# A new opening for a fused layer norm, long convolution and feed-forward kernel: first tile and first weights loaded first, roots on GpSimd, constant matmuls in early waits

## The chip, the cores and the metric

The kernel runs on one core of a Trainium2 chip. A core has five engines with queues of their own, each of which works strictly in the order in which instructions were put there: TensorE (PE: matmuls, with PEld for the loading of their weights), VectorE (DVE), ScalarE (ACT), GpSimd (POOL) and SyncE (SP, which here only issues DMAs). Engines wait for one another by semaphores. The metric is the device time of one execution in microseconds (us), the median of several.

## The reference

With S = 2048 rows, D = 1024 columns and F = 3584 hidden columns:

```python
x = A_q                                  # 2048 x 1024
xn = (x - mean(x)) / sqrt(var(x) + 1e-5) # per row
# branch A, per column of D
k_shift = causal_conv(k, shift_k)        # 4 taps
kv = k_shift * v
y = causal_conv(kv, ssm_k) + kv * ssm_D  # 2048 taps, by FFT in the reference
# branch B
h = silu(xn @ w1)                        # 2048 x 3584
return x + xn * y + h @ w2
```

All inputs and the output are float32.

## The kernel before, in words

Both products of branch B run on TensorE in float16, each operand split into a high and a low half, with three matmuls for each pair of blocks (high x high, high x low, low x high; `steps`, L959, and `steps2`, L1091). A split (`split`, L365) is two operations: ACT writes the high half (scaled, `a_act`, L350), and DVE subtracts it from the source and writes the low half (`v_stt`, L346). The first product uses Strassen-like sums of row and column quarters: an operand is either a plain quarter (A11, A12, A21, A22) or a sum of quarters (S1 to S4 for rows, T1 to T4 for weights). The convolution of branch A is done by Fourier matrices on TensorE, with the transforms in between on DVE, after the opening that concerns us here.

The rows come in 16 tiles of 128 rows. Tiles 0 to 3 are A11 and A12, tiles 4 to 7 are A21 and A22. A tile passes these steps:

- `load_row` (L503) loads it, the first two tiles in two pieces of 256 KB each.
- `ln_rows` (L512) takes statistics on DVE (two `bn_stats`, one `bn_aggr` per tile), the root of the variance on ACT (`AF.Sqrt`, L537), a chain of five small DVE operations that makes one refined reciprocal root (L530 to L534), and the norm itself, one DVE operation of 128x1024 per tile (L543). Statistics are taken for groups of 2, 2, 4 and 8 tiles before the group's root.
- `transposes` (L549) turns it on TensorE, four blocks of 128x128 into a PSUM tile of the ring `ft` (three tiles), and `first_rows`, `keep`, `lower_sums` and `upper_sums` split and add what came out, on ACT and DVE.

The weights w1 come in pairs of 256 hidden columns. `load_pair` (L711) loads one, `scales_w1` (L733) takes its sum of squares on ACT (`AF.Square` with an accumulator, into `junk`), adds the partitions by a matmul with ones (`total`, L444, PSUM tile `nm`), and makes powers of two from the sum as scales: for the first two pairs in a chain of six DVE operations (`norm`, L457, with `then`, L749), for the later ones with ACT adding up the columns, two DVE operations, and two small ACT operations for the scales (`norm_act`, L479). `factors_w1` (L781) splits the scaled weights into the places `wo`.

`feed_forward` (L1050) orders the matmuls. It begins with `plain_unit` (L970) for pair 0 with the upper rows, in two groups of two tiles (256 columns of the moving operand); then pair 1 with the upper rows, then pairs 0 and 1 with the lower rows, which need tiles 4 to 7 complete; then the units of sums. A SiLU on ACT takes each result out of PSUM. The SiLU and the root belong to different activation tables, and a change of table is an instruction of its own on ACT (`ACT_TABLE_LOAD`).

Nothing of this order is written out by hand. Each activity is a generator that yields operations (`Op`) with an engine, an estimated duration and a margin. `Order.run` (L165) keeps an estimated clock per engine and always emits the operation with the earliest estimated start, less a bias of its stream. The engines then run that order as emitted. A few matmuls with zeros (`op.fill`) are put into estimated TensorE gaps after 45 us of the estimate. The opening is set by `begin` (L1797): row tiles 0 and 1, weight pair 0, row tiles 2 and 3, pair 1, row tiles 4 to 7. `warm_up` (L1823) yields 26 matmuls of constants in float32, two records each in the profile, with an estimate of 0.44 us each, and holds a tile of the ring `ft` until they are emitted.

Of the kernel before, what the change touches and what calls it, by code (L numbers as in the profile page):

```python
# [11 lines left out]
F32 = mybir.dt.float32  # L12
# [8 lines left out]
P = 128  # L21
# [84 lines left out]
class Order:  # L106


# [56 lines left out]
    def run(self):  # L165
        while self.streams:
# [125 lines left out]
def h3_ffn_kernel(ctx, tc, x, kp, vs, fs, shift, dskip, w1, w2, cfwd, cinv, out):  # L292
# [151 lines left out]
    def total(ring, ss, n, margin):  # L444
# [7 lines left out]
        def mm():  # L452
            nc.tensor.matmul(pt[:, 0:n], onesb, high, start=True, stop=True)
        yield T(mm, pt[:, 0:n], [ss], 0.12, m=margin)
# [24 lines left out]
    def norm_act(ring, ss, ns, then, flags, margin=1.5):  # L479

        cols = len(ns)
        pt, tok, e, etok = yield from total(ring, ss, sum(ns), margin)
# [3 lines left out]
        tok.set()  # L486
        power, inverse = e[:, 0:cols], e[:, 2:2 + cols]

        def chain():
            nc.vector.tensor_scalar(power.bitcast(I32), power.bitcast(I32), 24, 23,  # L490
                                    op0=ALU.logical_shift_right, op1=ALU.logical_shift_left)
            nc.vector.reciprocal(inverse, power)
        yield V(chain, e, [power], us=0.33)
# [18 lines left out]
    def ln_rows():  # L512
        for t0, n, bias in ((0, 2, 0.26), (2, 2, 0.17), (4, 4, 0.15), (8, 8, 0.03)):
            yield bias
            q = slice(t0, t0 + n)
            mv = lnp.tile([P, 2, 8], F32, name="mv", bufs=2)
            m = mv[:, :, 0:n]
# [10 lines left out]
            def chain(m=m, q=q):  # L528
                v = stat[:, q, 1]
                nc.vector.reciprocal(m[:, 0, :], m[:, 0, :])  # L530
# [3 lines left out]
                nc.vector.tensor_mul(rstd[:, q], m[:, 0, :], m[:, 1, :])  # L534
# [4 lines left out]
            p.writes += [m[:, 0, :], m[:, 1, :]] + ([nmr] if n == 8 else [])  # L539
            yield p  # L540
            for t in order_in:
                xt = xts[t][0]
                yield V(lambda: nc.vector.tensor_scalar(xt, xt, stat[:, t, 0:1], rstd[:, t:t + 1], op0=SUB, op1=MUL),  # L543
# [189 lines left out]
    def scales_w1():  # L733
        for n, (_, i) in enumerate(pairs):
# [14 lines left out]
            def then(e, i=i):  # L749
                sc = wsc[:, i]  # L750
                nc.vector.tensor_scalar(sc[:, 3:5], powers[:, 3:5], e, None, op0=MUL)
                nc.vector.reciprocal(e, e)
                nc.vector.tensor_scalar(sc[:, 0:3], powers[:, 0:3], e, None, op0=MUL)

# [215 lines left out]
    def plain_unit(i, b, xf, ready, m=1, free=False):  # L970
# [921 lines left out]
```

## Time and profile before

| | |
|---|---|
| median of 3 runs | 1251.88 us (1251.4 to 1251.94) |
| profiled execution | 1250.78 us, span 1249.0 us |
| TensorE busy | 1227.0 us, 98% of the span |
| DVE busy | 1127.2 us, 90% |
| ACT busy | 749.5 us, 60% |
| GpSimd busy | 132.9 us, 11% |
| mean granted TensorE clock | 0.997 |

The span runs from the first to the last instruction of the profiled execution. A row of the profile in order of time reads: start, duration, engine, line of the kernel, operation, written tile <- read tiles, their shapes, how often in a row, and in brackets how long the engine had been idle before and who released it. A line is often that of a helper: L355 is every ACT operation, L347 every combined DVE operation, so the names of tiles tell more (`xt` row tiles, `x` places of the transposed rows and of the first weight pairs, `wo` split weights, `ff` results in PSUM, `mv` and `rstd` the root, `pow` and `wsc` the scales of w1, `junk` the squares).

### The profile page before, as it was taken

What the parts mean: (1) busy time and instruction counts of PE and PEld (TensorE: products, weight loads), DVE (VectorE), ACT (ScalarE), POOL (GpSimd) and SP (SyncE); (2) the same over time, 40 slices, a digit from 0 to 9 for tenths busy, and PEclk for the clock granted to TensorE, in tenths of its full rate; (3) what the DMA queues carried; (4) which work ended last, traced back from release to release, by engine and by line L of the source; (5) the groups of instructions that cost most, each with busy time, mean ns of one, the idle gap of its engine ahead of it and who ended that gap; (6) DMA issues with size and microseconds to landing.
All of it is one profiled execution on the core that took longest, in us unless ns stands there. A gap on an engine that the chain in (4) does not pass through costs nothing.

```text
span 1249.0 us, 17052 instructions
## 1 busy us (share of the span) xinstructions
PE 1227.0 (98%) x6017; PEld 591.7 (47%) x6017; DVE 1127.2 (90%) x1390; ACT 749.5 (60%) x1309; POOL 132.9 (11%) x141
## 2 busy tenths in 40 slices
PE   7899999999999999999999999999999999999998
PEld 6444544444444454445444544544454454445444
DVE  7999997889799979999899799889979979998992
ACT  6868897878767786757762632563273264526231
POOL 0000000000000030001110300310030030113114
PEclk8999999999999999999999999999999999999999
DMA  9358999889999898978998897689586587978766
GB/s 336 94 176 289 314 309 309 276 277 349 321 332 299 263 260 272 258 239 230 345 329 213 178 266 176 149 245 276 127 199 184 131 169 245 250 157 143 161 144 93
DMA packets 254293, 292.93 MB, mean 235 GB/s; under 512 B 48768, under 2 KB 167808, under 8 KB 252032
## 3 DMA queue, kind: packets, MB, share of 16 engines
q1 hardware_dynamic: 227472, 266.93, 67.4%
q0 software_dynamic: 26736, 24.92, 14.9%
q8 instruction: 47, 0.77, 0.2%
q14 instruction: 38, 0.31, 0.1%
HBM read 193.22 MB, written 98.57 MB: 234 GB/s over the span
## 4 chain that ended last, share of the span: by engine, by line
PE 69%; DVE 20%; issue 4%; DMA 4%; ACT 2%; POOL 0%; SPq 0%; DVEq 0%; POOLq 0%; ACTq 0%
PE ff L1096 10%; PE ff L1098 10%; PE ff L1097 10%; PE ff L966 10%; PE ff L964 10%; PE ff L965 10%; DVE spec L344 7%; DVE tmp L344 3%; DVE x L347 2%; PE ps L1563 2%; PE ps L1565 2%; PE ps L1564 2%; DVE spec L347 1%; DVE ht L347 1%; DMA out<-yt 1%
## 5 line engine op out<-in xcount | busy, mean ns | idle before, releaser
L1096 PE MATMUL ff<-x,wo 128*128 128x512 f16 x868 | 328.1, 378 | 1.0 <-DVE hf L347 0.6
L1098 PE MATMUL ff<-x,wo 128*128 128x512 f16 x868 | 328.1, 378 | 0.0
L1097 PE MATMUL ff<-x,wo 128*128 128x512 f16 x868 | 328.1, 378 | 0.0
L965 PE MATMUL ff<-x,wo 128*128 128x512 f16 (+1 forms) x808 | 303.9, 376 | 2.7 <-DVE x L347 2.7
L964 PE MATMUL ff<-x,wo 128*128 128x512 f16 (+1 forms) x808 | 303.9, 376 | 2.2 <-ACT wo L355 1.5
L966 PE MATMUL ff<-x,wo 128*128 128x512 f16 (+1 forms) x808 | 303.8, 376 | 1.7 <-DVE wo L347 0.9
L344 DVE TENSOR_TENSOR spec<-spec 128x1024 f32<-128x1024 f32 (+2 forms) x272 | 263.2, 1000 | 2.3
L1098 PEld LDWEIGHTS <-wo 128*128 128x128 f16 x868 | 84.9, 98 | 101.5
L1096 PEld LDWEIGHTS <-wo 128*128 128x128 f16 x868 | 84.9, 98 | 100.7
L1097 PEld LDWEIGHTS <-wo 128*128 128x128 f16 x868 | 84.9, 98 | 100.7 <-issue 1.4
L966 PEld LDWEIGHTS <-wo 128*128 128x128 f16 x808 | 79.4, 98 | 98.3 <-issue 3.3
L964 PEld LDWEIGHTS <-wo 128*128 128x128 f16 x808 | 79.4, 98 | 90.7 <-ACT wo L355 1.7
L965 PEld LDWEIGHTS <-wo 128*128 128x128 f16 x808 | 79.4, 98 | 88.5 <-issue 1.1
L341 POOL DMA_DIRECT2D out<-hf x59 | 52.2, 885 | 449.4 <-ACT hf L355 363.4
L355 ACT ACTIVATE hf<-ff,invc 128x512 f32<-128x512 f32 x60 | 40.9, 682 | 97.8 <-PE ff L1098 68.5
L341 POOL DMA_DIRECT2D out<-yt x56 | 63.1, 1327 | 333.1 <-DVE yt L347 189.6
L344 DVE TENSOR_TENSOR tmp<-spec 128x2048 f32<-128x2048 f32 (+1 forms) x48 | 92.6, 1934 | 0.9
L347 DVE SCALAR_TENSOR_TENSOR ht<-hf,wsc,ht 128x1024 f16<-128x1024 f32 (+1 forms) x56 | 67.3, 1204 | 12.5 <-ACT ht L355 12.4
L355 ACT ACTIVATE spec<-spec 128x1024 bf16<-128x1024 f32 x32 | 33.8, 1055 | 70.7 <-DVE spec L344 70.6
L347 DVE SCALAR_TENSOR_TENSOR wo<-raw,wsc,wo 128x512 f16<-128x512 f32 (+1 forms) x56 | 56.6, 1014 | 11.3 <-ACT wo L355 10.9
L355 ACT ACTIVATE spec<-ps 128x512 f32<-128x512 f32 x96 | 55.3, 590 | 16.6 <-PE ps L1565 14.9
L355 ACT ACTIVATE ht<-hf,wsc 128x1024 f16<-128x1024 f32 (+1 forms) x56 | 60.7, 1085 | 4.4 <-DVE hf L344 3.0
(173 smaller groups left out, 1753.6 us busy)
## 6 DMA issues: line engine op xcount, KB each, us to landing
wo<-hs SPq DMA_DIRECT2D x160, 256.0 KB, 3.7
hs<-ht SPq DMA_DIRECT2D x80, 256.0 KB, 4.6
wraw<-in_w SPq DMA_DIRECT2D x31, 512.0 KB, 5.3
out<-hf POOLq DMA_DIRECT2D x59, 256.0 KB, 4.3
raw<-in_w SPq DMA_DIRECT2D x28, 512.0 KB, 6.0
kin<-in_kp SPq DMA_DIRECT2D x16, 704.0 KB, 5.6
kf<-in_fs SPq DMA_DIRECT2D x8, 1024.0 KB, 5.3
hsfS<-ht SPq DMA_DIRECT2D x32, 256.0 KB, 4.5
```

Source lines behind the costliest of these rows:

```text
L341: return Op("POOL", 1.1, 4.8, lambda: nc.gpsimd.dma_start(o, i, accum_op=ADD), [i], [o], m, n)
L344: return V(lambda: nc.vector.tensor_tensor(o, a, b, op=op), o, [a, b], **k)
L347: return V(lambda: nc.vector.scalar_tensor_tensor(o, a, s, b, op0=op0, op1=op1), o, [a, b] + ([] if isinstance(s, float) else [s]), **k)
L355: nc.scalar.activation(o, i, func, scale=scale, **kw)
L964: nc.tensor.matmul(o, w[:, 0, k], xf[:, :, k, 0], start=first and k == 0, stop=False, **kw)
L965: nc.tensor.matmul(o, w[:, 0, k], xf[:, :, k, 1], start=False, stop=False, **kw)
L966: nc.tensor.matmul(o, w[:, 1, k], xf[:, :, k, 0], start=False, stop=last and k == KH - 1, **kw)
L1096: nc.tensor.matmul(o, hx[:, n, 0, :], wc[:, n, 0, q], start=first and n == 0, stop=False, **kw)
L1097: nc.tensor.matmul(o, hx[:, n, 0, :], wc[:, n, 1, q], start=False, stop=False, **kw)
L1098: nc.tensor.matmul(o, hx[:, n, 1, :], wc[:, n, 0, q], start=False, stop=last and n == 3, **kw)
L1563: nc.tensor.matmul(o, cf[:, 0], hi[i], start=i == 0, stop=False, **kw)
L1564: nc.tensor.matmul(o, cf[:, 0], lo[i], start=False, stop=False, **kw)
```

## The change

- **Loads.** `begin` loads row tile 0, then weight pair 0, then row tiles 1, 2 and 3. The rest is as before.
- **Row norms.** The groups are now 1, 1, 2, 4 and 8 tiles. The root and the five DVE operations are replaced by two GpSimd operations: add 1e-5, then raise to the power -0.5. For the groups of 2 and 4 two more GpSimd operations make -mean x rstd, and the tiles 3, 5 and 7 are normed by one ACT operation (`Identity` with scale and bias) in place of the DVE one.
- **Table.** No root is left on ACT, and the first activation loads the table of the SiLU.
- **Scales of w1.** Pairs 0 to 3 take `norm_act` with `joined`: TensorE also adds up the columns (a first matmul with 1e-32, then one for each column), so that neither DVE nor ACT has to, and the two DVE operations read PSUM directly. The margin of that matmul in the estimate goes from 1.5 to 0.5. Pairs 0 and 1 leave the DVE chain of six and get their scales from two ACT operations.
- **First unit.** `plain_unit` for pair 0 with the upper rows runs in groups of 1, 1 and 2 tiles (128, 128 and 256 columns) in place of 2 and 2.
- **Warm-up.** Its tile comes from the ring `ff`. The estimate for one warm-up matmul is 0.3 us. After the 26, every estimated gap of TensorE is filled with bfloat16 matmuls of constants of 512 columns (`order.spare`), until the first product has been emitted (`flag["first"]`).

```diff
@@ class Order, run
-            if op.fill is not None and t > 45.0:
+            if self.spare is not None and op.eng == "PE":
+                for _ in range(int((t - self.free["PE"] - 0.1) / 0.22)):
+                    self.spare()
+            elif op.fill is not None and t > 45.0:
@@ constants
+    tinyb = cst.tile([P, 1], BF16, name="tinyb")
+    nc.vector.memset(tinyb, 1e-32)
-    eps = cst.tile([P, 1], F32, name="eps")
-    nc.vector.memset(eps, 1e-5)
+    half = cst.tile([P, 1], F32, name="half")
+    nc.vector.memset(half, -0.5)
@@ def total(ring, ss, n, margin, joined=False):
         def mm():
-            nc.tensor.matmul(pt[:, 0:n], onesb, high, start=True, stop=True)
-        yield T(mm, pt[:, 0:n], [ss], 0.12, m=margin)
+            if joined:
+                nc.tensor.matmul(pt[:, 0:1], onesb, tinyb, start=True, stop=False)
+                for q in range(n):
+                    nc.tensor.matmul(pt[:, 0:1], onesb, high[:, q:q + 1], start=False, stop=q == n - 1)
+            else:
+                nc.tensor.matmul(pt[:, 0:n], onesb, high, start=True, stop=True)
+        yield T(mm, pt[:, 0:n], [ss], 0.12 + 0.04 * n * joined, m=margin)
@@ def norm_act(ring, ss, ns, then, flags, margin=1.5, joined=False):
-        for c, m in enumerate(ns):
+        for c, m in enumerate(() if joined else ns):
             o = pt[:, sum(ns[:c]):sum(ns[:c]) + m]
             yield a_act(o, o, AF.Copy, bias=1e-30, total=e[:, c:c + 1])
+        sums = pt[:, 0:cols] if joined else power
         def chain():
-            nc.vector.tensor_scalar(power.bitcast(I32), power.bitcast(I32), 24, 23,
+            nc.vector.tensor_scalar(power.bitcast(I32), sums.bitcast(I32), 24, 23,
                                     op0=ALU.logical_shift_right, op1=ALU.logical_shift_left)
             nc.vector.reciprocal(inverse, power)
@@ def ln_rows():
-        for t0, n, bias in ((0, 2, 0.26), (2, 2, 0.17), (4, 4, 0.15), (8, 8, 0.03)):
+        for t0, n, bias in ((0, 1, 0.26), (1, 1, 0.26), (2, 2, 0.17), (4, 4, 0.15), (8, 8, 0.03)):
             def chain(m=m, q=q):
-                v = stat[:, q, 1]
-                nc.vector.reciprocal(m[:, 0, :], m[:, 0, :])
-                nc.vector.tensor_mul(m[:, 1, :], m[:, 0, :], m[:, 0, :])
-                nc.vector.scalar_tensor_tensor(m[:, 1, :], v, 1e-5, m[:, 1, :], op0=ADD, op1=MUL)
-                nc.vector.tensor_scalar(m[:, 1, :], m[:, 1, :], -0.5, 1.5, op0=MUL, op1=ADD)
-                nc.vector.tensor_mul(rstd[:, q], m[:, 0, :], m[:, 1, :])
-                if n == 8:
-                    nc.vector.scalar_tensor_tensor(nmr, stat[:, :, 0], -1.0, rstd, op0=MUL, op1=MUL)
-            yield a_act(m[:, 0, :], stat[:, q, 1], AF.Sqrt, bias=eps)
-            p = V(chain, rstd[:, q], [stat[:, q, :], m[:, 0, :]], us=0.8)
+                nc.gpsimd.tensor_scalar(m, stat[:, q, 1], 1e-5, None, op0=ADD)
+                nc.gpsimd.tensor_tensor(rstd[:, q], m, power, op=ALU.pow)
+                if n in (2, 4):
+                    nc.gpsimd.tensor_scalar(m, stat[:, q, 0], -1.0, None, op0=MUL)
+                    nc.gpsimd.tensor_tensor(nmr[:, q], m, rstd[:, q], op=MUL)
+            power = half.to_broadcast([P, n])
+            p = V(chain, rstd[:, q], [stat[:, q, :]], us=1.2)
+            p.eng = "POOL"
+            if n in (2, 4):
+                p.busy += 0.5
             yield p
+            if n == 8:
+                yield V(lambda: nc.vector.scalar_tensor_tensor(nmr, stat[:, :, 0], -1.0, rstd, op0=MUL, op1=MUL),
+                        nmr, [stat, rstd])
             for t in order_in:
                 xt = xts[t][0]
+                if t in (3, 5, 7):
+                    yield a_act(xt, xt, AF.Identity, rstd[:, t:t + 1], nmr[:, t:t + 1])
+                    flag["xn", t].set()
+                    continue
@@ def scales_w1():
-            if n < 2:
-                yield from norm(ctxs["nm"], ss[:, 0:m], (m,), then, ([wsc[:, i]], [flag["scaled", n], tok]))
-            else:
-                yield from norm_act(ctxs["nm"], ss[:, 0:m], (m,), scales, [flag["scaled", n], tok])
+            early = n < 4
+            yield from norm_act(ctxs["nm"], ss[:, 0:m], (m,), scales, [flag["scaled", n], tok],
+                                0.5 if early else 1.5, early)
@@ def feed_forward():
-        yield from plain_unit(0, 0, first, (r, r), 2)
+        yield from plain_unit(0, 0, first, (r, r), (1, 2, 4))
@@ def begin():
-        for t in (0, 1):
-            yield from load_row(t)
+        yield from load_row(0)
         yield from load_pair(0)
-        for t in (2, 3):
+        for t in (1, 2, 3):
             yield from load_row(t)
@@ def warm_up():
-        pt, tok = ft.tile([P, KH, P])
+        pt, tok = ff.tile([P, 4, P])
         for _ in range(26):
-            yield T(lambda: nc.tensor.matmul(pt[:, 0, :], ones, ones, start=True, stop=True), pt[:, 0, :], [], 0.44)
+            yield T(lambda: nc.tensor.matmul(pt[:, 0, :], ones, ones, start=True, stop=True), pt[:, 0, :], [], 0.3)
+        def constants():
+            nc.tensor.matmul(pt.rearrange("p a b -> p (a b)"), onesb, oneb.to_broadcast([P, W]), start=True, stop=True)
+        order.spare = constants
+        yield flag["first"]
+        order.spare = None
         tok.set()
@@ start
-    nc.scalar.activation(warm, ones[:, 0:1], AF.Sqrt)
+    nc.scalar.activation(warm, ones[:, 0:1], AF.Silu)
+    order.table = AF.Silu
```

More of the change, by code (lines that the diff above doesn't have):

```diff
@@ L106 @@
 class Order:
+    spare = None
     def __init__(self):
@@ L477, in norm, with norm_act @@
             t.set()
-    def norm_act(ring, ss, ns, then, flags, margin=1.5):
+    def norm_act(ring, ss, ns, then, flags, margin=1.5, joined=False):
         cols = len(ns)
-        pt, tok, e, etok = yield from total(ring, ss, sum(ns), margin)
-        for c, m in enumerate(ns):
+        pt, tok, e, etok = yield from total(ring, ss, sum(ns), margin, joined)
+        for c, m in enumerate(() if joined else ns):
             o = pt[:, sum(ns[:c]):sum(ns[:c]) + m]
             yield a_act(o, o, AF.Copy, bias=1e-30, total=e[:, c:c + 1])
-        tok.set()
+        if not joined:
+            tok.set()
         power, inverse = e[:, 0:cols], e[:, 2:2 + cols]
+        sums = pt[:, 0:cols] if joined else power
         def chain():
-            nc.vector.tensor_scalar(power.bitcast(I32), power.bitcast(I32), 24, 23,
+            nc.vector.tensor_scalar(power.bitcast(I32), sums.bitcast(I32), 24, 23,
                                     op0=ALU.logical_shift_right, op1=ALU.logical_shift_left)
             nc.vector.reciprocal(inverse, power)
-        yield V(chain, e, [power], us=0.33)
+        yield V(chain, e, [sums], us=0.33)
+        if joined:
+            tok.set()
         yield from then(power, inverse)
@@ L968, in steps, with plain_unit @@
                     skip_group_check=more)
-    def plain_unit(i, b, xf, ready, m=1, free=False):
+    def plain_unit(i, b, xf, ready, ends=(4,), free=False):
         ph = []
@@ L975, in plain_unit @@
             ph.append(ff.tile([P, 4, P]))
-        for n, j in [(n, j) for n in range(m) for j in range(2)]:
-            q = slice(n * 4 // m, (n + 1) * 4 // m)
+        for q, j in [(slice(([0] + list(ends))[n], e), j) for n, e in enumerate(ends) for j in range(2)]:
+            last = q.stop == 4
             for a in range(2):
-                for r in ready[a][n * len(ready[a]) // m:(n + 1) * len(ready[a]) // m]:
+                for r in ready[a] if len(ends) == 1 else ready[a][q]:
                     yield r
@@ L983, in plain_unit @@
                 yield from steps(ph[j][0][:, q, :], w, xf[a][:, q], a == 0, a == 1)
-                if free and n == m - 1:
+                if free and last:
                     tok.set()
-            if n == m - 1:
+                flag["first"].set()
+            if last:
                 if j == 0:
```

14 lines of the change are left out of this document (5 added, 9 removed).

## The prediction

> **What bounds the kernel now.** I read the page's shares first, then the busy time by stretches of the span, then the order of time in the first 54 us, then the groups of ScalarE (ACT) there.
>
> ```profile
> PE 1227.0 (98%) x6017; PEld 591.7 (47%) x6017; DVE 1127.2 (90%) x1390; ACT 749.5 (60%) x1309; POOL 132.9 (11%) x141
> ```
>
> Busy time of each engine in five stretches that I cut at the places the argument needs (columns: stretch, its length, then PE, PEld, DVE, ACT, POOL busy with instructions, granted clock, DMA share, GB/s), and two finer ones:
>
> ```profile
> 0.00:13.10 13.10, 9.49 (x65) 9.16 (x65) 7.39 (x26) 6.00 (x14) 0.69 (x6) 1.00 0.84 290
> 13.10:53.90 40.80, 31.80 (x206) 21.26 (x207) 37.41 (x81) 34.71 (x65) 0.00 (x0) 0.92 0.66 230
> 53.90:550.00 496.10, 495.78 (x2367) 231.76 (x2367) 451.11 (x580) 381.21 (x636) 11.46 (x11) 1.00 0.88 281
> 550.00:1200.00 650.00, 646.19 (x3143) 306.54 (x3142) 604.46 (x675) 314.98 (x576) 103.44 (x107) 1.00 0.80 208
> 1200.00:1249.00 49.00, 43.69 (x239) 23.00 (x236) 26.85 (x33) 12.57 (x20) 17.32 (x18) 0.99 0.67 108
> 15.00:20.00 5.00, 2.73 (x13) 1.64 (x14) 4.51 (x9) 4.42 (x10) 0.00 (x0) 0.54 1.03 419
> 20.00:25.00 5.00, 5.00 (x38) 4.20 (x37) 4.51 (x14) 2.17 (x5) 0.00 (x0) 0.78 1.02 406
> ```
>
> From 53.9 to 1200 us TensorE idles 0.32 + 3.81 = 4.1 us in 1146. So the end is, to a first reading, the moment at which TensorE starts to run without gaps, plus a fixed amount of matmul work. The opening is different: to 53.9 us TensorE idles 3.6 + 9.0 us, 8 us of the rest are warm-up matmuls, and around 15 to 22 us its clock is granted at half. What it waits for is ACT and VectorE (DVE):
>
> ```profile
> 1.07 7.99 PE L1827 MATMUL ft<-one 128*128 128x128 f32 x52 [1.07 <-DVE one L395]
> 10.90 1.50 PE L562 MATMUL ft<-ident,xt 128*128 128x128 f32 x12 [1.84 <-issue]
> 12.24 0.17 PE L453 MATMUL nm<-ss,oneb 128*128 128x4 bf16 x1
> 16.36 0.40 PE L964 MATMUL ff<-x,wo 128*128 128x256 f16 x1 [1.48 <-ACT wo L355]
> 20.84 0.42 PE L965 MATMUL ff<-x,wo 128*128 128x256 f16 x1
> 21.06 0.42 PE L966 MATMUL ff<-x,wo 128*128 128x256 f16 x1
> 22.60 0.27 PE L966 MATMUL ff<-x,wo 128*128 128x256 f16 x1
> 22.71 0.27 PE L964 MATMUL ff<-x,wo 128*128 128x256 f16 x1
> 53.99 0.38 PE L965 MATMUL ff<-x,wo 128*128 128x512 f16 x1 [0.67 <-DVE x L347]
> ```
>
> The last row is the start of the gapless part: the first product with the lower rows (tiles 4 to 7), held up by their last split on DVE. The first useful matmul is at 16.36. In the stretch 13.1 to 53.9 DVE is busy 37.4 of 40.8 us and ACT 34.7, so both queues are nearly full, and ACT's 6.1 us of idle time are these two groups' (columns: instructions, busy, mean | idle before, releaser):
>
> ```profile
> L355 ACT ACTIVATE x<-ft 128x512 f16<-128x512 f32 x14 | 8.2, 601 | 4.2 <-PE nm L453 2.8 <-DVE s L344 1.3
> L355 ACT ACTIVATE xt<-ft 128x512 f32<-128x512 f32 x8 | 4.7, 602 | 1.8 <-DVE x L347 1.8
> L355 ACT ACT_TABLE_LOAD x3 | 3.8, 1283 | 0.1
> L355 ACT ACTIVATE junk<-x 128x1024 bf16<-128x1024 f32 x2 | 2.1, 1050 | 0.0
> L355 ACT ACTIVATE ht<-hf,wsc 128x1024 f16<-128x1024 f32 x1 | 1.2, 1151 | 0.0
> L355 ACT ACTIVATE mv<-stat,eps 128x2 f32<-128x2 f32 (+1 forms) x2 | 0.6, 290 | 0.0
> ```
>
> **The change, part by part.** I price it at one place: how much earlier the 53.99 row comes.
>
> *Loads.* Each queue entry stays; only SP's order changes. Row tile 1 (two 256 KB pieces) moves behind the four pieces of the w1 pair, and everything after these keeps its place.
>
> ```profile
> 3.48 0.69 DVE L524 BATCH_NORM_STATS2 st<-xt 128x6 f32<-128x512 f32 x1 [2.38 <-DMA xt<-in_x]
> 6.29 1.40 DVE L524 BATCH_NORM_STATS2 st<-xt 128x6 f32<-128x512 f32 x2 [0.99 <-DMA xt<-in_x]
> 8.05 0.63 ACT L355 ACTIVATE junk<-x 128x512 bf16<-128x512 f32 x1 [5.81 <-DMA x<-in_w]
> 9.79 0.16 DVE L534 TENSOR_TENSOR rstd<-mv 128x2 f32<-128x2 f32 x1
> 10.90 0.19 ACT L355 ACTIVATION_READ_ACCUMULATOR junk<-x 128x1 f32 x1
> ```
>
> The third piece now lands at 6.29, the fifth at 8.05. So w1 is there from about 6.3 on, and four squares of 0.8 us (0.63 + 0.19) end near 9.7 where they ended at 11.1. Tile 1 lands two to three us later and is normed about a microsecond later than now, tile 0 three earlier.
>
> *First matmul.* Tile 0 is normed by about 7.1, but the 26 warm-ups still hold TensorE until 9.06. The plan believes 0.3 us each, so 7.8 in all, and puts some constant matmuls of 0.22 us before the first product (no row shows how many; I take ten, from a planned gap of some 2 us). Transposes of tile 0 (8 of 0.125 us, from the row of twelve) then end near 10.6, the sum (five small matmuls for the one at 12.24) near 11.0, its two DVE operations near 11.4, two scales on ACT at 11.9, the first split at 12.6. The first product starts at about 12.7, 3.6 us earlier; constants issued too late cost up to 1.3 of it.
>
> *Clock.* Two neighbours at half clock start 0.22 us apart, two at full clock 0.11. From about 17.9 to 22.1 some 20 matmuls pay 0.10 each: 2.1 us. I count them as saved, since the constants fill the wait before 12.7 and later waits of 1 us left the clock at 1.00. The Trainium skill, "TensorE: Matmul & The Clock Gate", Parts 1 and 4, says an idle window of some 3.4 us halves the clock and that transposes do not count as activity; the 0.54 above, after a stretch with only transposes, agrees. It puts matmuls of 128 columns in a stream at some 81 ns; by that the 96 of the next step would cost 2.5 us more than 48 of 256.
>
> *Smaller first groups.* Plain unit 0 now runs over 1, 1 and 2 tiles: 96 matmuls of 128 columns in place of 48 of 256. If a half costs half (0.055 us), nothing is added; if the spacing stays 0.109, 96 x 0.055 = 5.3 us are. I take 4, near the upper end, since one weight load already lasts 0.10 us. It is covered: TensorE's useful work from the first product to the lower rows is 96 x 0.09 + 48 x 0.109 + 48 x 0.2155 + 7 tiles' transposes 7 + 0.8 = some 32 us, so it could be there at 45, and waits for ACT and DVE until later than that. Without that cover its 4 us come back in full.
>
> *DVE from 13.1 to 53.9.*
>
> ```profile
> 13.46 0.15 DVE L466 TENSOR_REDUCE pow<-nm 128x1 f32<-128x4 f32 x1
> 14.48 0.23 DVE L753 TENSOR_SCALAR wsc<-powers,pow 128x3 f32<-128x3 f32 x1
> 20.37 0.15 DVE L530 RECIPROCAL mv<-mv 128x2 f32<-128x2 f32 x1
> 21.15 0.16 DVE L534 TENSOR_TENSOR rstd<-mv 128x2 f32<-128x2 f32 x1
> 35.66 0.18 DVE L530 RECIPROCAL mv<-mv 128x4 f32<-128x4 f32 x1 [0.89 <-ACT mv L355]
> 36.67 2.98 DVE L543 TENSOR_SCALAR xt<-xt,stat,rstd 128x1024 f32<-128x1024 f32 x4
> 40.23 0.15 DVE L490 TENSOR_SCALAR pow<-pow 128x1 int32<-128x1 int32 x1
> 40.41 0.16 DVE L492 RECIPROCAL pow<-pow 128x1 f32<-128x1 f32 x1
> ```
>
> Two w1 chains of six operations (13.46 to 14.71, 1.25 us) become two operations (0.34): 2 x 0.9 = 1.8 us off. Two root chains (20.37 to 21.31, 0.95 us) go to GpSimd: 1.9 off. Norms of tiles 3, 5 and 7 (2.98 / 4 each) go: 2.2 off. Together 5.9 us, 6.8 if the wait of 0.89 for the root on ACT goes and no wait for GpSimd takes its place.
>
> *ACT from 13.1 to 53.9.* Off: three table loads (3.85), two roots (0.58), and the sum of pair 2 (about 0.34). On: three norms of 128x1024, 1.05 to 1.15 us by the two rows above, 3.4; two scales for pair 1, 0.46. Net only 0.9 us off. So ACT is the queue that decides. With its idle time unchanged it ends 0.9 us earlier; with none, 7.0. The 2.8 us behind "PE nm" come from TensorE working off tile 0 and 1 late and at half clock; they mostly go. The other 3.1 wait for DVE, which loses six times more work than ACT; I take a half off. 0.9 + 2.3 + 1.5 = 4.7, and 0.5 for a slightly earlier state at 13.1.
>
> *GpSimd.* Its chain (two operations, four where the shift is needed too) stands between statistics and norm four times; the power appears in no row. Rows nearest:
>
> ```profile
> 1.02 0.29 POOL masks.py:199 TENSOR_SCALAR_AFFINE_SELECT ident<-ident 128x128 f32<-128x128 f32 x1
> 204.11 0.95 POOL L341 DMA_DIRECT2D kf<-in_dskip  x1 [202.81 <-DMA ws_T<-wo]
> ```
>
> Per chain 0.2 us (two memset-like steps) to 4 us (four steps like the longest). I take the plan's own 1.2, near the lower row, since the operands are one to eight elements wide; DVE's removed chain with the root's wait took 1.0 to 2. Its queue is empty until 204 us. 0.7 us of new waits in the three chains after tile 0 are my term. The eight-tile chain comes at about 108 us, where ACT has room.
>
> *The rest.* Moving the warm-up tile to the other bank ring, the start value of the sums and the smaller scratch cost nothing: unit 1 needs the third and fourth bank only 20 us later. Past 53.9 the next producers stand close:
>
> ```profile
> 72.47 2.49 DVE L347 SCALAR_TENSOR_TENSOR wo<-raw,wsc,wo 128x1024 f16<-128x1024 f32 x2
> ```
>
> These splits end at 75.0. Two units of 48 matmuls (0.2155 each, 20.7 us) and the first product of the next put their use at 77 or later. DVE moves forward at least as far as TensorE, so this holds.
>
> Sum: 4.7 + 0.5 - 0.7 = 4.5 us at the 53.99 row, and from there TensorE passes it to the end. The profiled execution took 1250.78 us (span 1249.0 and 1.8 around it), 1.1 under the median of 1251.88: 1246.3 for such an execution, **1247.4 us** for the median.
>
> **Rivals.**
>
> A, more: ACT's idle time vanishes and DVE's 6.8 us come through: 7 us, 1245.0. For it: both queues are work-bound. Against: in-order queues with an order planned from estimates keep some waits.
>
> B, the change does little: the warm-ups and late constants hold tile 0, ACT gets three norms for three table loads, its waits stay: 0.9 + 0.5 us, 1250.5. For it: ACT's net of 0.9. Against: the 2.8 us behind a half-clocked TensorE.
>
> C, slower: the GpSimd chain. If each of the three chains after tile 0 takes 4 us with DVE stopped behind it, 3 x (4 - 1.2) = 8.4 us are lost against the 4.5: 1255.8. It turns slower by 0.2% when a chain passes some 3.5 us. The Trainium skill, "GPSIMD Engine Reference", sections 1 and 8, says GpSimd shares its SBUF interfaces with VectorE and collides with two-input or 2-port instructions; by it each step could wait for a DVE instruction. In this kernel those last 0.7 us, so four steps add 2.8 per chain, and with the steps themselves it nears that point. Against it: operands of few elements. No row here shows the two engines at work together.
>
> D, slower: the planner lays out everything after from its running estimates, so the whole later order shifts. Waits after 53.9 sum to 4.1 us today, and a new order has to add 7 for a loss of 0.2%: 1255. Such waits (1.5 and 1.7 us) exist at the convolution's first stage, but two or three times as many are unlikely.
>
> **Chances.** Forecast 0.54 (its own range 1245.8 to 1249.3); A 0.13; B 0.14; C 0.10; D 0.09. A measurement tells about 0.2% (2.5 us) from no change: faster is forecast and A, 0.67; same is B, 0.14; slower is C and D, 0.19. The range 1244.5 to 1252.5 holds forecast, most of A and B, and leaves C and D out.
>
> **What would show it.** The first product at about 12.7; clock 1.00 from 15 to 25; one table load in all; 128-column matmuls 0.08 to 0.11 us apart; GpSimd chains near 1.2 us with little DVE idle time behind them; the first lower-row product at about 49.5; 4 us of TensorE waits after it. Wrong it would be if ACT's waits stay at 6 us, if DVE waits over 2 us for a root, or if the waits past 54 us grow by more than 2.

## The result, and the profile after

| | before | after |
|---|---|---|
| median of 9 runs each | 1251.94 us | 1248.34 us |
| ratio of the runs, with its 95% interval | | 0.9970 (0.9957 to 0.9983) |
| profiled execution's span | 1249.0 us | 1247.7 us |

The change made the kernel 3.6 us faster by the medians. 1247.4 us was forecast. A second measurement of the same kernel, beside the experiments (again, below), gave 0.9959 (0.9946 to 0.9972), some 5 us. Single executions lie up to 2 to 5 us from their median, so the profiled spans alone don't tell kernels apart by less than that.

Shares of the span, then busy time by stretches cut at the same places as before (columns as above: PE, PEld, DVE, ACT, POOL, clock, DMA share, GB/s):

```profile
PE 1230.0 (99%) x6089; PEld 593.7 (48%) x6089; DVE 1120.0 (90%) x1360; ACT 744.7 (60%) x1303; POOL 142.6 (11%) x155
```

```profile
0.00:13.10 13.10, 12.04 (x80) 10.31 (x81) 5.50 (x21) 6.89 (x16) 2.31 (x10) 1.00 0.85 294
13.10:53.90 40.80, 35.30 (x285) 23.90 (x284) 37.31 (x69) 34.30 (x63) 5.40 (x8) 1.00 0.65 222
53.90:550.00 496.10, 495.85 (x2372) 231.65 (x2370) 450.11 (x577) 379.84 (x636) 14.21 (x13) 1.00 0.89 284
550.00:1200.00 650.00, 644.41 (x3126) 305.40 (x3125) 601.54 (x664) 311.05 (x570) 103.91 (x107) 1.00 0.81 206
1200.00:1247.70 47.70, 42.36 (x232) 22.42 (x230) 25.52 (x33) 12.58 (x20) 16.77 (x17) 1.00 0.68 105
15.00:20.00 5.00, 2.82 (x42) 2.29 (x39) 4.96 (x10) 4.96 (x10) 0.00 (x0) 1.00 1.02 405
20.00:25.00 5.00, 4.32 (x69) 4.33 (x70) 4.13 (x10) 2.42 (x5) 1.94 (x4) 1.00 1.03 402
```

To 53.9 us TensorE idles 1.1 + 5.5 us in place of 3.6 + 9.0, at full clock. Some 4 us of this are the constants, which count as busy: without them (noconst, below) it idles 3.2 + 5.2. From 550 to 1200 it idles 5.6 us in place of 3.8: part of the lead was given back there. The main steps of the opening, in order of time on TensorE:

```profile
8.86 1.25 PE L1847 MATMUL ff<-oneb 128*128 128x512 bf16 x5
9.95 1.04 PE L586 MATMUL ft<-ident,xt 128*128 128x128 f32 x8
10.95 3.44 PE L1847 MATMUL ff<-oneb 128*128 128x512 bf16 x15
14.26 1.09 PE L586 MATMUL ft<-ident,xt 128*128 128x128 f32 x8
15.19 0.22 PE L981 MATMUL ff<-x,wo 128*128 128x128 f16 x1
15.24 0.22 PE L982 MATMUL ff<-x,wo 128*128 128x128 f16 x1
18.98 0.23 PE L981 MATMUL ff<-x,wo 128*128 128x128 f16 x1 [1.41 <-ACT wo L360]
20.68 0.23 PE L983 MATMUL ff<-x,wo 128*128 128x128 f16 x1 [1.41 <-DVE wo L352]
26.91 0.66 PE L586 MATMUL ft<-ident,xt 128*128 128x128 f32 x4 [1.43 <-ACT xt L360]
36.30 0.66 PE L586 MATMUL ft<-ident,xt 128*128 128x128 f32 x4 [0.37 <-ACT xt L360]
48.45 0.38 PE L981 MATMUL ff<-x,wo 128*128 128x512 f16 x1
48.82 0.38 PE L982 MATMUL ff<-x,wo 128*128 128x512 f16 x1
```

The 20 constants stand in two groups, before the transposes of tile 0 and before those of tile 1. The first product is at 15.19 (before: 16.36). The last two rows are the 49th and 50th matmul of 512 columns, the first two with the lower rows; before, the 50th was the row at 53.99. So that row came 5.2 us earlier, and no wait stands in it any more: after 36.3 TensorE runs on without a wait worth naming. In what follows "the lower-row mark" is the 49th, the first of the two: 52.95 before, 48.45 after.

Read up to the 50th product, from 13.1 us on, the two kernels compare like this (busy and idle time in us, from the stretches 13.1 to 53.99 and 13.1 to 48.82):

| | before | after |
|---|---|---|
| length | 40.9 | 35.7 |
| ACT busy, idle | 34.8, 6.1 | 29.3, 6.5 |
| DVE busy, idle | 37.5, 3.4 | 32.2, 3.5 |
| TensorE busy, idle | 31.8, 9.1 | 30.2, 5.5 |

Both queues have over 5 us less work in front of that product, and as much idle time as before. ACT's idle time only changed its causes. Before, it waited 2.8 us for TensorE's sum (`nm`) and 3.1 for DVE; after, 3.8 us for GpSimd's shift (`nmr`, rows below), 1.6 for DVE's `pow` and 1.1 for other DVE work.

GpSimd's chains, and the ACT norms that wait for them:

```profile
5.15 0.24 POOL L545 TENSOR_SCALAR mv<-stat 128x1 f32<-128x1 f32 x1 [3.85 <-DVE stat L542]
5.48 0.58 POOL L546 TENSOR_TENSOR rstd<-mv,half 128x1 f32<-128x1 f32 x1
21.15 0.71 POOL L546 TENSOR_TENSOR rstd<-mv,half 128x2 f32<-128x2 f32 x1
21.95 0.80 POOL L548 TENSOR_SCALAR mv<-stat 128x2 f32<-128x2 f32 x1
22.83 0.20 POOL L549 TENSOR_TENSOR nmr<-mv,rstd 128x2 f32<-128x2 f32 x1
31.25 0.62 POOL L545 TENSOR_SCALAR mv<-stat 128x4 f32<-128x4 f32 x1 [8.23 <-DVE stat L542]
31.95 1.39 POOL L546 TENSOR_TENSOR rstd<-mv,half 128x4 f32<-128x4 f32 x1
33.43 0.80 POOL L548 TENSOR_SCALAR mv<-stat 128x4 f32<-128x4 f32 x1
34.31 0.65 POOL L549 TENSOR_TENSOR nmr<-mv,rstd 128x4 f32<-128x4 f32 x1
97.52 2.06 POOL L546 TENSOR_TENSOR rstd<-mv,half 128x8 f32<-128x8 f32 x1
```

```profile
23.06 1.24 ACT L360 ACTIVATE xt<-xt,nmr,rstd 128x1024 f32<-128x1024 f32 x1 [1.01 <-POOL nmr L549]
35.00 2.38 ACT L360 ACTIVATE xt<-xt,nmr,rstd 128x1024 f32<-128x1024 f32 x2 [2.79 <-POOL nmr L549]
```

For tile 0 the root takes 0.9 us, for the group of 4 it takes 2.1 (31.25 to 33.34), and 3.7 with the shift.

### The profile page after: what moved, and what is told of

The parts are those of the page before. It is cut to its first block, busy times and chain, and to the rows that moved or that the text cites. A ratio compares the mean times of both kernels' runs of the same rounds, so it can differ in the third digit from the quotient of the medians.

```text
span 1247.7 us, 17185 instructions
## 1 busy us (share of the span) xinstructions
PE 1230.0 (99%) x6089; PEld 593.7 (48%) x6089; DVE 1120.0 (90%) x1360; ACT 744.7 (60%) x1303; POOL 142.6 (11%) x155
## 4 chain that ended last, share of the span: by engine, by line
PE 70%; DVE 18%; DMA 5%; issue 3%; ACT 2%; POOL 0%; SPq 0%; DVEq 0%; ACTq 0%
PE ff L981 10%; PE ff L982 10%; PE ff L983 10%; PE ff L1114 10%; PE ff L1116 10%; PE ff L1115 10%; DVE spec L349 6%; DVE tmp L349 2%; PE ps L1581 2%; PE ps L1583 2%; PE ps L1582 2%; DVE x L352 2%; DVE ht L352 1%; DMA wraw<-in_w 1%; DVE hf L349 1%
## 5 line engine op out<-in xcount | busy, mean ns | idle before, releaser
L981 PE MATMUL ff<-x,wo 128*128 128x512 f16 (+2 forms) x824 | 304.1, 371 | 1.6 <-ACT wo L360 1.4
L983 PE MATMUL ff<-x,wo 128*128 128x512 f16 (+2 forms) x824 | 304.1, 371 | 1.5 <-DVE wo L352 1.4
L982 PE MATMUL ff<-x,wo 128*128 128x512 f16 (+2 forms) x824 | 304.1, 371 | 0.7 <-DVE x L352 0.7
L360 ACT ACTIVATE hf<-ff,invc 128x512 f32<-128x512 f32 x60 | 40.9, 681 | 100.2 <-PE ff L1116 74.8
L352 DVE SCALAR_TENSOR_TENSOR ht<-hf,wsc,ht 128x1024 f16<-128x1024 f32 (+1 forms) x56 | 67.2, 1203 | 12.8 <-ACT ht L360 12.7
```

What stands on the lines that cost most here:

```text
L352: return V(lambda: nc.vector.scalar_tensor_tensor(o, a, s, b, op0=op0, op1=op1), o, [a, b] + ([] if isinstance(s, float) else [s]), **k)
L360: nc.scalar.activation(o, i, func, scale=scale, **kw)
L981: nc.tensor.matmul(o, w[:, 0, k], xf[:, :, k, 0], start=first and k == 0, stop=False, **kw)
L982: nc.tensor.matmul(o, w[:, 0, k], xf[:, :, k, 1], start=False, stop=False, **kw)
L983: nc.tensor.matmul(o, w[:, 1, k], xf[:, :, k, 0], start=False, stop=last and k == KH - 1, **kw)
```

## The experiments

Each starts from the changed kernel. Ratios are against the kernel before, measured beside it. "Idle later" is TensorE's idle time from 53.9 to 1200 us in the profiled execution, worked out from the rows of the stretches. The clock is the granted one from 15 to 20 and from 20 to 25 us. The 50th product is listed beside the mark, because in four kernels filling matmuls of zeros stand right ahead of the mark and can hold it by themselves (6 in before, 10 in nmrdve, 8 each in oldroots and oldloads; none in the others). Each run has one profile.

| kernel | lower-row mark | 50th product | clock | idle later | ratio (95% interval) |
|---|---|---|---|---|---|
| before | 52.95 | 53.99 | 0.54, 0.78 | 4.1 | 1 |
| after | 48.45 | 48.82 | 1.00, 1.00 | 5.8 | 0.9970 (0.9957 to 0.9983) |
| again | 49.59 | 49.96 | 1.00, 0.68 | 5.2 | 0.9959 (0.9946 to 0.9972) |
| noconst | 48.33 | 48.70 | 0.77, 1.00 | 4.7 | 0.9956 (0.9940 to 0.9972) |
| late16 | 52.89 | 53.11 | 1.00, 0.66 | 3.7 | 0.9989 (0.9976 to 1.0002) |
| nmrdve | 48.92 | 49.78 | 1.00, 1.00 | 6.0 | 0.9997 (0.9985 to 1.0008) |
| actplus | 50.28 | 51.12 | 1.00, 1.00 | 6.5 | 0.9982 (0.9967 to 0.9996) |
| dveplus | 50.77 | 51.39 | 1.00, 1.00 | 4.2 | 0.9994 (0.9980 to 1.0008) |
| oldroots | 52.68 | 53.62 | 1.00, 0.56 | 11.0 | 1.0061 (1.0040 to 1.0083) |
| oldloads | 50.12 | 51.06 | 1.00, 1.00 | 5.5 | 1.0000 (0.9988 to 1.0012) |
| slower_plan | 49.41 | 49.77 | 1.00, 0.66 | 4.7 | 0.9983 (0.9971 to 0.9995) |
| faster_plan | 48.94 | 49.30 | 1.00, 1.00 | 3.6 | 0.9948 (0.9936 to 0.9960) |
| groups22 | 48.02 | 48.38 | 1.00, 1.00 | 5.0 | 0.9951 (0.9937 to 0.9964) |
| normsdve | 48.39 | 48.60 | 1.00, 0.66 | 7.7 | 0.9969 (0.9957 to 0.9981) |

**again.** No edit.

> The changed kernel once more, unaltered, as the base of the others on this chip. Its first lower-row products started at 48.45 and 48.82 us, 5.2 us before the old ones; between 600 and 700 us TensorE then waited 2.5 and 1.0 us for ACT. Theory 1 (those waits belong to the new order of instructions): they come again at the same place with 2 us or more, and the gain over the kernel before stays near 3.6 us. Theory 2 (they are chance of one execution, a late transfer for instance): they are gone or elsewhere in this profile, the span is near 1244.5, and the gain of the profiled execution is near 5.

Neither theory as stated. In this execution the waits between 550 and 1200 us were 4.1 us. The longer of the two at 600 to 700 us came again at the same place but shorter (1.9 us in place of 2.5, at 694), so it belongs to the order; the one of 1.0 us did not come again. More telling is the opening, the same instructions in the same order:

```profile
20.00:25.00 5.00, 4.49 (x55) 4.49 (x56) 4.13 (x10) 2.33 (x4) 1.94 (x4) 0.68 1.02 403
```

Here the clock did fall, and the mark came at 49.59.

**noconst.** The constants are not emitted; the order of all else is kept.

```diff
-        order.spare = constants
+        order.spare = lambda: None
```

> The 20 constant matmuls are left out, everything else keeps its order on every engine. Prediction's theory: the clock falls to half between about 14 and 20 us, as before the change; the 128-column products of tiles 0 and 1 then start 0.107 us apart in place of 0.056, some 2 to 4 us of TensorE time, part of it hidden behind ACT and DVE. The first lower-row product comes 0.5 to 2 us later than 48.45, and so does the end. Rival (TensorE has slack in the opening): the clock falls, but the first lower-row product stays within 0.3 us of 48.45 and the time within 0.5 us of the base.

The clock falls earlier (0.77 from 15 to 20 us) and not after 20; the mark is at 48.33 and the ratio is that of the base. The rival holds: the constants are worth nothing here. Among the seven profiles with the constants and this opening (after, again, late16, actplus, dveplus, slower_plan, faster_plan) the clock fell in three, between 20 and 25, in the waits behind the first products. The three are those whose first product started earliest (14.82, 14.84 and 15.02 us); in the other four it started between 15.19 and 15.68. No run shows whether that is the cause.

```profile
15.00:20.00 5.00, 4.04 (x44) 3.63 (x42) 4.97 (x10) 4.83 (x10) 0.00 (x0) 0.77 1.03 405
20.00:25.00 5.00, 4.45 (x70) 4.45 (x71) 4.13 (x10) 2.55 (x5) 1.94 (x4) 1.00 1.02 404
48.33 0.38 PE L981 MATMUL ff<-x,wo 128*128 128x512 f16 x1
```

**late16.** Sixteen constants ahead of the lower-row mark, order kept.

```diff
-                yield from steps(ph[j][0][:, q, :], w, xf[a][:, q], a == 0, a == 1)
+                more = steps(ph[j][0][:, q, :], w, xf[a][:, q], a == 0, a == 1)
+                if i == 0 and b == 1 and j == 0 and a == 0:
+                    op = next(more)
+                    def idle(emit=op.emit):
+                        for _ in range(16):
+                            nc.tensor.matmul(ph[0][0].rearrange("p a b -> p (a b)"), onesb,
+                                             oneb.to_broadcast([P, W]), start=True, stop=True)
+                        emit()
+                    op.emit = idle
+                    yield op
+                yield from more
```

> Sixteen matmuls of constants of 512 columns (0.2155 us each, 3.45 us) are put directly ahead of the first lower-row product, into the bank that this product then starts afresh; the order is kept. It takes 3.4 us of the lead away at one place. Prediction's theory (what TensorE has there is passed to the end): the first lower-row product at about 51.9 and the end 3.4 us later than the base, so about even with the kernel before. Rival (a later stage bound by DVE or transfers takes up the lead): the end moves by less than 1.5 us.

The mark moved to 52.89, 3.3 us past that of the base with the same fall of the clock. The end moved by 0.9989 - 0.9959, 0.3% or 3.7 us, with some 0.2% of uncertainty. So with the order kept, what TensorE gains or loses at the mark is passed to the end, as forecast.

```profile
52.89 0.38 PE L981 MATMUL ff<-x,wo 128*128 128x512 f16 x1
```

**nmrdve.** The shift by DVE in place of GpSimd.

```diff
-                if n in (2, 4):
-                    nc.gpsimd.tensor_scalar(m, stat[:, q, 0], -1.0, None, op0=MUL)
-                    nc.gpsimd.tensor_tensor(nmr[:, q], m, rstd[:, q], op=MUL)
...
+            yield p
             if n in (2, 4):
...
+                yield V(lambda: nc.vector.scalar_tensor_tensor(nmr[:, q], stat[:, q, 0], -1.0, rstd[:, q], op0=MUL, op1=MUL),
+                        nmr[:, q], [stat[:, q, :], rstd[:, q]], us=0.2)
```

> -mean x rstd of tile groups 2 and 4 is made by one DVE operation of 2 or 4 elements (0.16 us) in place of two GpSimd operations, which took 0.80 and 0.20 us in the group of 2 and 0.80 and 0.65 us in the group of 4; the later order changes with it. In the changed kernel ACT waited 1.01 us and 2.79 us for them. If these waits are on the path: ACT's wait for the group of 4 shrinks to about 1.3 us, the first lower-row product comes 1 to 2 us earlier than 48.45, and the end too. If DVE decides: no change of the first lower-row product within 0.5 us.

```profile
33.89 2.37 ACT L360 ACTIVATE xt<-xt,nmr,rstd 128x1024 f32<-128x1024 f32 x2 [1.36 <-DVE nmr L553]
47.15 0.38 PE L980 MATMUL ff<-x,wo 128*128 128x512 f16 x1
47.80 1.28 PE L332 MATMUL ff<-one,zero 128*128 128x128 f32 x10
48.92 0.38 PE L978 MATMUL ff<-x,wo 128*128 128x512 f16 x1
49.78 0.38 PE L979 MATMUL ff<-x,wo 128*128 128x512 f16 x1 [0.48 <-DVE x L352]
L332 PE MATMUL ff<-one,zero x22: 272/273/422, 47.8 to 614.3; 128*128 128x128 f32 x22
```

ACT's wait fell from 2.79 to 1.36 us, and the mark did not move (48.92 against 48.45 and, in faster_plan, 48.94, all at full clock). That alone proves little, since ten matmuls of zeros stand right ahead of the mark here. The rows around it say more. The 48th product, the row at 47.15, came 1.1 us earlier than in the change (48.24), so ACT's shorter wait did let TensorE move ahead. But the 50th, at 49.78, came 1.0 us later than there and waited for DVE's last split. With ACT relieved, DVE held the lower rows, and the lead was not used. Yet the end is 4 to 5 us worse than the base. The later order was laid anew by the planner, with 22 filling matmuls of zeros in place of 4 and 6.0 us of idle time later.

**actplus, dveplus.** One small operation of each lower sum made twice, on ACT or on DVE, order kept.

```diff
 # actplus: the copy c21 <- a21 on ACT
-        yield a_act(c21, a21, AF.Copy)
+        p = a_act(c21, a21, AF.Copy)
+        if ring is s1_r:
+            def twice(emit=p.emit):
+                emit()
+                emit()
+            p.emit = twice
+        yield p
 # dveplus: the addition s1 <- a22 + c21 on DVE
-        yield v_tt(s1, a22, c21, ADD)
+        def add_rows():
+            for _ in range(2 if ring is s1_r else 1):
+                nc.vector.tensor_tensor(s1, a22, c21, op=ADD)
+        yield V(add_rows, s1, [a22, c21])
```

> The copy on ACT at the head of each of the four lower sums (128x512, 0.58 us, between 38 and 47 us) is made twice; the order is kept. 4 x 0.48 = 1.9 us more work for ACT. Prediction's theory (ACT is the queue that sets the first lower-row product): that product 1.5 to 1.9 us later than the base's 48.4 to 49.6, and the end 1.5 us or more later. Rival (TensorE itself sets it, since it runs without a gap from 36.8 us on in the changed kernel): the product moves by less than 0.7 us, the end by less than 0.7.

> The DVE addition of each of the four lower sums (128x512, 0.60 us apart, between 38 and 49 us) is made twice; the order is kept. 2.4 us more work for DVE. If DVE set the first lower-row product: it comes 2 us or more later than 48.4 to 49.6. Prediction's theory (ACT): less than 1 us. Rival (TensorE): less than 0.7 us, and the end within 0.7 us of the base.

```profile
50.28 0.38 PE L987 MATMUL ff<-x,wo 128*128 128x512 f16 x1 [0.51 <-ACT x L360]
```

```profile
50.77 0.38 PE L984 MATMUL ff<-x,wo 128*128 128x512 f16 x1
```

Against 48.45 to 48.94 at full clock, 1.9 us more of ACT cost 1.3 to 1.8 us at the mark and 2.4 us more of DVE cost 1.8 to 2.3. So neither "ACT decides" nor "TensorE decides" stands. Work added to any of the three queues shows nearly in full (for TensorE, 3.3 of 3.45 us in late16). An estimate from these differences is that each has less than about 0.6 us of slack at the mark. Relieving one of them alone (nmrdve) brought the lower rows no earlier.

**oldroots.** Root on ACT and five DVE operations again, in the new groups.

```diff
-                nc.gpsimd.tensor_scalar(m, stat[:, q, 1], 1e-5, None, op0=ADD)
-                nc.gpsimd.tensor_tensor(rstd[:, q], m, power, op=ALU.pow)
+                nc.vector.reciprocal(m[:, 0, :], m[:, 0, :])
...
+                if n in (2, 4):
+                    nc.vector.scalar_tensor_tensor(nmr[:, q], stat[:, q, 0], -1.0, rstd[:, q], op0=MUL, op1=MUL)
-            p = V(chain, rstd[:, q], [stat[:, q, :]], us=1.2)
-            p.eng = "POOL"
+            yield a_act(m[:, 0, :], stat[:, q, 1], AF.Sqrt, bias=eps)
+            p = V(chain, rstd[:, q], [stat[:, q, :], m[:, 0, :]], us=0.8)
...
-    nc.scalar.activation(warm, ones[:, 0:1], AF.Silu)
+    nc.scalar.activation(warm, ones[:, 0:1], AF.Sqrt)
...
```

> The roots go back to ACT (Sqrt) and the five DVE operations, in the new groups of 1, 1, 2, 4 and 8, with -mean x rstd by DVE; all else as changed, the later order is laid anew. Prediction's theory: DVE gets 4 chains of about 0.95 us before 54 us back and ACT the roots and at least three table loads of 1.28 us (3.8 us in all on ACT); first lower-row product 2.5 to 4 us later than the base, end 2 to 4 us later. Rival (TensorE sets the opening, table loads fall into ACT's waits): less than 1.5 us at that product.

```profile
52.68 0.38 PE L983 MATMUL ff<-x,wo 128*128 128x512 f16 x1
550.00:1200.00 650.00, 639.04 (x3095) 302.76 (x3094) 590.31 (x647) 305.53 (x565) 102.17 (x105) 1.00 0.81 205
PE ps L1583 <- ACT tmp L360: 4.8, 3, 2.5
PE ps L1583 <- DVE tmp L349: 1.6, 1, 1.6
```

The mark is back at 52.68: 3.1 us behind the base with a fallen clock, 4.2 behind the one without. By the 50th product (53.62), which waited for DVE and not for the zeros, it is 3.7 and 4.8. The order of the opening was laid anew here too, so the figure holds that as well. Of the parts that were taken back singly, the root's way is the largest. Only one further table load fell before 54 us (at 35.09), not three, so the count behind the expectation was wrong. The end is 7.6 us worse than before, which the opening doesn't explain: 11.0 us of waits stand later, the largest of them at the convolution's first stage (last two rows: waiter, releaser, total, times, longest).

**oldloads.** Row tile 1 ahead of weight pair 0 again.

```diff
         yield from load_row(0)
+        yield from load_row(1)
         yield from load_pair(0)
-        for t in (1, 2, 3):
+        for t in (2, 3):
```

> Row tile 1 is loaded ahead of weight pair 0 again; all else as changed, the later order is laid anew. Prediction's theory: the squares of pair 0 end 1.4 us later, tile 1 is normed about 1 us earlier; first product about 1 us later or even, first lower-row product within 1 us of the base: the load order is worth little by itself. Rival (the load order carries the gain): the first lower-row product comes 2 us or more later.

The mark is at 50.12, 1.2 to 1.7 us late at full clock, and the 50th product at 51.06, 1.8 to 2.2 us late: between the two expectations, by the 50th product close to the rival. The load order carries a part of the gain. The end gave back all of the remaining lead of 2.8 us, again under a new later order.

**slower_plan, faster_plan.** The planner's estimates after 60 us of its clock times 1.01 or 0.99; the opening stays the same.

```diff
+            if t > 60.0:
+                op.busy *= 1.01   # or 0.99
             done = t + op.busy
```

> The changed kernel; only the planner's estimate of each operation's duration after 60 us of its clock is 1% longer, so the opening is the same instruction for instruction and the order after it is laid anew. Theory 1 (the order after the opening is worth microseconds by itself, which is where the kernels with an equal lead and different ends got theirs): first lower-row product between 48.4 and 49.6 as in the base, the end 2 us or more away from the base's 1248.1, on either side. Theory 2 (the end is the opening plus a fixed amount): the end within 1 us of the base.

> The same with the estimates after 60 us 1% shorter: a second draw of the later order. Theory 1: first lower-row product between 48.4 and 49.6, the end 2 us or more from the base's 1248.1. Theory 2: within 1 us.

```profile
48.94 0.38 PE L983 MATMUL ff<-x,wo 128*128 128x512 f16 x1
53.90:550.00 496.10, 496.06 (x2371) 231.29 (x2370) 446.06 (x577) 379.73 (x632) 14.19 (x13) 1.00 0.89 285
550.00:1200.00 650.00, 646.45 (x3138) 306.11 (x3137) 606.76 (x666) 313.68 (x578) 104.24 (x108) 1.00 0.81 206
```

These rows are of faster_plan. Their ratios, 0.9983 and 0.9948, have intervals that don't meet: 0.35% or 4.4 us between two orders laid over the same opening (medians 1250.02 and 1245.98 us). About 0.5 us of it is the clock in the opening of the profiled executions. So between these two Theory 1 holds: the order after the opening is worth microseconds by itself. Against the base (1248.12 us) each is 1.4 to 3 us off, by medians or by ratios, which is less than twice the uncertainty.

**groups22.** The first unit in two groups of two tiles.

```diff
-        yield from plain_unit(0, 0, first, (r, r), (1, 2, 4))
+        yield from plain_unit(0, 0, first, (r, r), (2, 4))
```

> The first unit runs in groups of two and two tiles (256 columns) again; the order of DVE, ACT and the DMA queue is kept. In the changed kernel products of 128 columns started 0.056 us apart, half of 0.109, so the small groups cost nothing and this edit saves nothing there. If starting on tile 0 alone helps: first product later than 15.2, first lower-row product 0.5 us or more later. Rival (no use, since the weight splits set the pace from 15 to 21 us): first lower-row product within 0.4 us of 48.4 to 49.6, the end within 0.7 us of 1248.1.

```profile
18.04 0.27 PE L981 MATMUL ff<-x,wo 128*128 128x256 f16 x1
48.02 0.38 PE L981 MATMUL ff<-x,wo 128*128 128x512 f16 x1
```

The first product comes 2.9 us later than in the change, behind 33 constants in place of 20, and the mark at 48.02 is no later. The rival holds: the early start on tile 0 is used up in the two waits of 1.41 us for weight splits at 18.98 and 20.68. With the two-tile groups TensorE had no wait from 18.04 to 24 us.

**normsdve.** All norms on DVE, no shift from GpSimd.

```diff
-                if n in (2, 4):
+                if n in ():
                     nc.gpsimd.tensor_scalar(m, stat[:, q, 0], -1.0, None, op0=MUL)
                     nc.gpsimd.tensor_tensor(nmr[:, q], m, rstd[:, q], op=MUL)
...
-                if t in (3, 5, 7):
+                if t in ():
```

> Tiles 3, 5 and 7 are normed on DVE again (0.75 us each) and the two GpSimd operations for the shift go; all else as changed, the later order is laid anew. ACT loses 3.6 us of norms and its waits of 1.0 and 2.8 us for GpSimd, DVE gets 2.2 us. If the moved norms are part of the gain: first lower-row product 1 us or more later than 48.4 to 49.6. If moving them to ACT was worth nothing: within 0.7 us, or earlier. The end is expected to differ by what the later order makes of it, so the verdict goes by that product.

The mark is at 48.39 although the clock fell: a microsecond earlier than in the kernels of the change's opening with a fallen clock (49.41 and 49.59), and the 50th product is 1.2 to 1.4 us earlier. Moving three norms to ACT gained nothing in the opening; by this one profile it lost about 1 us. At the end 7.7 us of idle time later take it back.

## Why the prediction was right, point by point

- **The place and the sum.** "TensorE passes it to the end" held where the order was kept (late16). The row at 53.99 was forecast 4.5 us earlier, at about 49.5; it came 5.2 us earlier in the after profile (48.82), and the row ahead of it, the mark, 4.5 us there and 3.4 in again, whose clock fell. The end followed with 3.6 us in the one measurement and 5 in the other. The number was right, several of its terms were not, and part of the agreement is luck.
- **ACT's idle time, 3.8 of 6.1 us to go.** This was the largest term of the sum, and it failed. The 2.8 us behind "PE nm" did go and the waits for DVE shrank somewhat, but ACT then waited 3.8 us for GpSimd's shift, so its idle time up to the 50th product is 6.5 us. "ACT's waits stay at 6 us" was named as a sign of being wrong, and it came. What shrank is the work ahead of the product: ACT did 5.5 us less between 13.1 us and that product, not 0.9. Three table loads and the roots went and three norms came, as forecast. But two squares of a later weight pair with their reads (2.5 us), a SiLU (0.7) and the ACT halves of two splits (1.3) now stand behind the product, and 0.9 us more of ACT's work stands ahead of 13.1. The sum priced no such move. An estimate from the groups of both profiles is that the replaced operations alone took some 0.3 us off ACT; the rest is the new order.
- **First matmul, 12.7.** Wrong: 15.19. The first product stands behind the transposes of tile 1 on TensorE (14.26), and these stand behind 15 constants and wait for tile 1's norm. It cost nothing, as groups22 shows with a first product at 18.04.
- **Clock, 2.1 us saved by the constants.** This step failed. noconst, without them, has the same mark and time. The clock fell in three of seven profiles of this opening in spite of them, at a later place. A clock that fell there cost about 0.8 us at the mark (49.4 and 49.6 against 48.4 to 48.9).
- **Smaller groups, 4 us taken as covered.** Mis-sized: 128-column products started 0.056 us apart, half of 0.109, so nothing was added. The Trainium skill's 81 ns, from "TensorE: Matmul & The Clock Gate", was not seen either; the same page's 55.6 ns for a warm stream agrees with this row.
- **DVE, 5.9 to 6.8 us off; ACT, 0.9 us off.** DVE did 5.3 us less between 13.1 us and the 50th product, near the forecast, though there too some operations changed places with the new order. oldroots puts 3.1 to 4.8 us on the way of the root, its new order included. "So ACT is the queue that decides" failed: actplus and dveplus cost nearly alike, and with less waiting (nmrdve) or fewer norms (normsdve) on ACT the 50th product came 1.0 us later or 0.2 earlier than in the change. TensorE, ACT and DVE were nearly balanced there. The two-operation scales of w1 (1.8 us of the DVE term) were not taken back singly, so their share stays open.
- **GpSimd, 1.2 us per chain, 0.7 us of new waits.** The chain was about right for widths 1 and 2 (0.9 and 1.0 us to the root), too small for the group of 4: 2.1 us, and 3.7 with the shift. The new waits were larger: 1.3 us on DVE (0.36 and 0.94, rows below) and 3.8 on ACT, which the term left out. Rival C's mechanism is there, but no engine stood 4 us behind a chain. Taking 1.4 us off ACT's wait of 2.79 did not bring the lower rows earlier (nmrdve).
- **Rival D.** Underrated. I held two or three times the 4.1 us of later waits to be unlikely. Of the kernels here they reached 7.7 and 11.0 us, and at nearly the same lead the end differed by more than 5 us: faster_plan and nmrdve have the mark at 48.94 and 48.92 and ratios of 0.9948 and 0.9997. That the change itself fell on an ordinary order was not something that the forecast had argued.

## What to carry to other kernels

Where a planner lays the order from running estimates, judge an edit in the opening by a mark at the end of the opening and by the end, separately: the end holds the redrawn order as well, here worth as much as the edit, and a small change of late estimates draws another order cheaply (faster_plan, 1245.98 us, is faster than both kernels). Before a queue is named the bound, add a microsecond or two to each of the candidates with the order kept; with balanced queues, relieving one can show nothing, because the next one then holds. Read the rows around a mark too: what stands right ahead of it may be a filler. Matmuls that only keep TensorE busy help only where a fall of the clock costs time. Here the fall ahead of 20 us (noconst) cost nothing at the mark, and the one behind the first products, which came in three of seven profiles in spite of the constants, cost about 0.8 us.

## What the runs showed of the hardware

The power on GpSimd took 0.58, 0.71, 1.39 and 2.06 us for 1, 2, 4 and 8 elements a partition, the last two partly beside DVE operations. The same narrow `TENSOR_SCALAR` took 0.22 to 0.24 us with DVE idle (1 and 2 elements) and 0.62 to 0.80 beside a DVE operation (2 to 8 elements). In two cases it ended with that operation:

```profile
21.90 0.81 DVE L567 TENSOR_SCALAR xt<-xt,stat,rstd 128x1024 f32<-128x1024 f32 x1 [0.36 <-POOL rstd L546]
33.38 1.53 DVE L567 TENSOR_SCALAR xt<-xt,stat,rstd 128x1024 f32<-128x1024 f32 x2 [0.94 <-POOL rstd L546]
```

The GpSimd row at 21.95 ends at 22.75, DVE's at 22.71; the one at 33.43 ends at 34.23, the first of DVE's two at about 34.15. That agrees with what the Trainium skill says in "GPSIMD Engine Reference", section 8, of interfaces shared with VectorE; no run here took the contention away. The multiply at 22.83 took only 0.20 us while DVE ran `BATCH_NORM_STATS2`, so not every DVE operation slows GpSimd. The clock fell or stayed for the same instructions in the same order, so it depends on something that the order of instructions doesn't set.
